# A linear attention and channel mix kernel: v cast on ScalarE, a shorter token mix, 0.5 in the relu scale, and ordered weight transfers

## The chip, the cores and the metric

The kernel runs on one core of a Trainium2 chip. The metric is the device time of one execution in microseconds (us), and what is quoted is the median of several executions. The engines are TensorE (PE in the profile, with its weight loads as PEld), VectorE (DVE), ScalarE (ACT), GpSimd (POOL) and SyncE (SP); beside them sixteen DMA engines move data.

## The reference

An efficient attention is computed for each of 8 batches and 8 heads (576 tokens, head size 64). Its output, seen as 576 x 512, goes through a channel mix that blends each token with the one before it.

```python
q_s = softmax(q, axis=-1)              # over the 64 features of a token
k_s = softmax(k, axis=2)               # over the 576 tokens
kv  = einsum('bhsd,bhse->bhde', k_s, v)
x   = einsum('bhsd,bhde->bhse', q_s, kv)          # then to (8, 576, 512)

x_prev = shift_by_one_token(x)                    # zeros in front
xk = mu_k * x + (1 - mu_k) * x_prev
xr = mu_r * x + (1 - mu_r) * x_prev
k  = relu(xk @ w_k)                               # 512 -> 1024
v  = (k * k) @ w_v                                # 1024 -> 512
r  = sigmoid(xr @ w_r)
out = r * v
```

Inputs and outputs are float32.

## The kernel before

One batch is worked in two half batches of four heads each: `attention(b, g)`. The channel mix runs in 12 units of 384 tokens: `unit(n)`. Both are generators, and the main loop interleaves them, so that TensorE works on unit n while the other engines prepare later batches. Unit 0 needs batch 0 alone; unit 1 reads tokens 384 to 767 and so needs all of batch 1 too.

Three parts matter here. First, who issues the transfers, and in which order: q, k and v from SyncE, the weights from GpSimd.

```python
def emit_load(b, g):
    t = ldpool.tile([128, 3, 2, J * D], F32, tag="raw", name="raw")
    for i, src in enumerate((q, k, v)):
        ap = ...
        nc.sync.dma_start(out=t[:, i, :, :], in_=ap)
    raw[b, g] = t

def emit_weights():
    for dst, src, n in ((wk_bf, moe_w_k, F), (wr_bf, moe_w_r, C)):
        ...                                              # four pieces each
        nc.gpsimd.dma_start(out=dst[...], in_=ap)
    for h in range(2):
        ...
        nc.gpsimd.dma_start(out=wv_h, in_=ap)
        nc.vector.tensor_scalar(out=wv_h, in0=wv_h, scalar1=0.5, scalar2=None,
                                op0=ALU.mult)
```

Second, the attention of a half batch: a cast of v on GpSimd, exps on ScalarE, the products on TensorE, and the mix on VectorE.

```python
nc.gpsimd.tensor_copy(out=vv[...], in_=t[:, 2, ...])          # v: f32 -> bf16
for i in (1, 0):                                              # k, then q
    nc.scalar.activation(out=eqk[:, i, ...], in_=t[:, i, ...], func=ACT.Exp)
# ... row sums of q, qs = q / sum; kvp = k^T v on TensorE; w = kvp / z, masked
# ... qtp = qs transposed; xp = w^T qt, one half (hf) after the other:
nc.scalar.copy(out=xb[:, hf, 64:64 + S].rearrange(...), in_=xp[:, :, 0:288])
# ... the mix, once for xk and once for xr (m):
for hf in range(2):
    c = 4 * m + 2 * g + hf
    nc.vector.tensor_scalar(out=xm[:, hf, :], in0=xb[:, hf, 64:64 + S],
                            scalar1=mu[:, c:c + 1], scalar2=None, op0=ALU.mult)
    nc.vector.tensor_scalar(out=xq[:, hf, :], in0=xb[:, hf, 0:S],
                            scalar1=om[:, c:c + 1], scalar2=None, op0=ALU.mult)
nc.vector.tensor_tensor(out=dst[...], in0=xm[:], in1=xq[:], op=ALU.add)
```

Third, a unit, and the order of the start:

```python
# in unit(n), for each of 8 column groups: four k matmuls, relu, square
nc.scalar.activation(out=rel[:], in_=kfp[:, 0:U], func=ACT.Relu)
nc.vector.tensor_tensor(out=k2[:, fc, :], in0=rel[:], in1=rel[:], op=ALU.mult)
# then three tiles of 128 tokens: rp (4 matmuls), tanh(0.5 rp), vp (8 matmuls), and
nc.vector.scalar_tensor_tensor(out=ot[:], in0=th[:], scalar=1.0, in1=vp[:],
                               op0=ALU.add, op1=ALU.mult)
# ... (sigmoid(r) = (1 + tanh(r / 2)) / 2: the halving sits in w_v)

# start (the loads of batch 0 were emitted earlier)
a0 = attention(0, 0); next(a0)
a1 = attention(0, 1); next(a1)
emit_weights()
emit_mu()
emit_load(1, 0)
emit_load(1, 1)
```

The softmax here doesn't subtract the row's maximum and nothing guards it: scores larger than these inputs give would overflow.

## Time and profile before

| | before |
|---|---|
| median of 3 executions | 246.61 us (246.5 to 248.75) |
| span of the profiled execution | 244.5 us |
| TensorE busy | 190.5 us, 78% |
| VectorE busy | 186.2 us, 76% |
| ScalarE busy | 120.0 us, 49% |
| GpSimd busy | 33.8 us, 14% |

These shares are averages over three quite different stages. The first lines are from the profile page of the kernel before: busy time per engine, and then two rows of the picture in 40 slices of about 6.1 us, in which each digit is the busy share in tenths (9 is 90% or more).

```profile
PE 190.5 (78%) x1296; PEld 103.2 (42%) x1313; DVE 186.2 (76%) x434; ACT 120.0 (49%) x197; POOL 33.8 (14%) x32
...
PE   0335200898987969797979999979999999999992
...
DVE  1489312999999999999999999999969844252521
```

TensorE is nearly idle for seven slices, to about 44 us: this is the start-up (stage 1). Then VectorE is full and TensorE has gaps (stage 2). From about 190 us TensorE alone is full (stage 3). The same in numbers, from the view that sums the engines' busy time over chosen stretches of the kernel before. A row has the stretch and its length, the busy time of each engine with its number of instructions, the granted TensorE clock as a share of full speed, the DMA share (it adds up packets that overlap, so it can pass 1) and GB/s.

```profile
core 0: us, PE busy (x) PEld busy (x) DVE busy (x) ACT busy (x) POOL busy (x), PEclk, DMA share, GB/s
24.00:44.00 20.00, 1.80 (x22) 1.38 (x23) 6.23 (x15) 5.72 (x6) 2.29 (x2) 0.57 1.11 321
...
110.00:130.00 20.00, 17.14 (x116) 9.06 (x118) 19.81 (x46) 11.83 (x19) 2.29 (x1) 1.00 0.77 249
200.00:213.00 13.00, 12.95 (x69) 6.69 (x69) 4.93 (x11) 5.72 (x11) 0.00 (x0) 1.00 0.26 61
```

In the middle (110 to 130) VectorE is 99% busy and TensorE 86%. Near the end a unit takes 13 us with TensorE at 100%. From 24 to 44 us no engine is half busy.

What the start-up waits for is read from the chain of waits of the kernel before: the work that ended last, followed back from the end, each row with its start, its length, its engine and its tile. These are its rows up to the first long run of k matmuls.

```profile
4.47 9.44 DMA raw<-in_v_dram
...
13.97 2.21 POOL vv_104 L146
16.18 0.54 POOL wk_bf L109
16.72 2.37 POOL wr_bf L109 x4
19.09 0.70 POOL wv_bf L117
19.79 21.27 DMA wv_bf<-in_moe_w_v_dram
...
41.09 0.69 DVE wv_bf L118
...
43.28 0.68 DVE xk L210
...
44.00 3.49 PE kfp L222 x11
```

The end of this chain: the second half of w_v lands, VectorE multiplies it by 0.5, and only then mixes the token rows that the first matmuls need. Its beginning: a cast of v (`vv_104`) that stood waiting for data. Rows "POOL wk_bf", "wr_bf" and "wv_bf" are GpSimd issuing transfers.

The timeline of VectorE in the kernel before shows the wait itself. A row has start, length, engine, line, operation, output and input, count, and in brackets the idle time before it and what ended that.

```profile
35.54 0.69 DVE L118 TENSOR_SCALAR wv_bf<-wv_bf 128x2048 bf16<-128x2048 bf16 x1 [8.28 <-DMA wv_bf<-in_moe_w_v_dram]
41.09 0.69 DVE L118 TENSOR_SCALAR wv_bf<-wv_bf 128x2048 bf16<-128x2048 bf16 x1 [4.85 <-DMA wv_bf<-in_moe_w_v_dram]
...
85.47 1.25 DVE L208 TENSOR_SCALAR xq<-xb_110,om 128x576 bf16<-128x576 bf16 x1
```

VectorE stood 8.28 + 4.85 = 13.1 us for 1.4 us of work. The last row is of stage 2: a scaling that takes 0.36 us elsewhere took 1.25 us, beside a cast of v on GpSimd that began at 85.28.

### The profile page before, as it was taken

The page shows a single profiled execution, that of the slowest core. Times are in us where ns is not written, and L with a number is a line of the kernel's source. Part 1 is how long each engine was busy: PE and PEld are TensorE (multiplying, and loading weights), DVE is VectorE, ACT ScalarE, POOL GpSimd, SP SyncE. Part 2 cuts the span into 40 slices and gives each one's busy share as a digit, 9 for nine tenths or more (in the row PEclk, how much of TensorE's full clock was granted, in tenths as well). Part 3 has the DMA queues.
Part 4 walks back from the last instruction along what each step waited for, and adds up shares of the span by engine and source line. Part 5 has one row for each costly group of instructions (what it writes and reads, how often), then busy time and mean ns, then how long its engine had stood idle before and what let it go on. Part 6 is the DMA issues. An engine that isn't in the chain of part 4 may idle for free.

```text
span 244.5 us, 3656 instructions
## 1 busy us (share of the span) xinstructions
PE 190.5 (78%) x1296; PEld 103.2 (42%) x1313; DVE 186.2 (76%) x434; ACT 120.0 (49%) x197; POOL 33.8 (14%) x32
## 2 busy tenths in 40 slices
PE   0335200898987969797979999979999999999992
PEld 0223200453543545453544555534655545454540
DVE  1489312999999999999999999999969844252521
ACT  4351520495292755465383774741734626162620
POOL 2375011610112010110110140100000000000000
PEclk9999655699999999999999999999999999999997
DMA  6999999921997587898881303203113031322313
GB/s 224 368 319 314 298 293 357 394 86 25 254 333 292 130 315 230 252 298 268 260 285 44 86 3 79 51 4 86 43 39 92 0 90 43 73 55 51 81 43 86
DMA packets 21065, 40.60 MB, mean 166 GB/s; under 512 B 2104, under 2 KB 3640, under 8 KB 21048
## 3 DMA queue, kind: packets, MB, share of 16 engines
q1 hardware_dynamic: 18816, 37.76, 49.4%
q0 software_dynamic: 2208, 2.62, 6.1%
q8 instruction: 10, 0.16, 0.3%
q14 instruction: 7, 0.06, 0.1%
q10 hardware_dynamic: 24, 0.00, 0.0%
HBM read 33.56 MB, written 9.44 MB: 176 GB/s over the span
## 4 chain that ended last, share of the span: by engine, by line
PE 49%; DVE 27%; DMA 14%; ACT 4%; POOL 2%; issue 1%; DVEq 0%; ACTq 0%
PE vp L239 21%; PE kfp L222 14%; PE rp L232 9%; DMA wv_bf<-in_moe_w_v_dram 9%; DVE qs L160 5%; DVE xq L208 4%; DMA raw<-in_v_dram 4%; DVE xm L206 3%; PE xp L192 2%; DVE xr L210 2%; DVE xk L210 2%; DVE rsum L156 2%; DVE ot L242 2%; ACT eqk L150 2%; PE qtp L182 2%; DMA raw<-in_q_dram 2%
## 5 line engine op out<-in xcount | busy, mean ns | idle before, releaser
L222 PE MATMUL kfp<-xk,wk_bf 128*128 128x384 bf16 x384 | 69.4, 331 | 15.9 <-DVE xk L210 15.1
L226 ACT ACTIVATE rel<-kfp 128x384 bf16<-128x384 f32 x96 | 46.1, 495 | 38.0 <-PE kfp L222 32.5
L222 PEld LDWEIGHTS <-wk_bf 128*128 128x128 bf16 x384 | 37.3, 99 | 40.0 <-issue 16.9
L150 ACT ACTIVATE eqk<-raw 128x1152 bf16<-128x1152 f32 x32 | 36.7, 1163 | 34.5 <-DMA raw<-in_q_dram 15.1
L242 DVE SCALAR_TENSOR_TENSOR ot<-th,vp 128x512 f32<-128x512 f32 x36 | 24.5, 684 | 21.7 <-PE vp L239 18.6
L235 ACT ACTIVATE th<-rp 128x512 f32<-128x512 f32 x36 | 21.6, 599 | 33.8 <-PE rp L232 33.5
L232 PE MATMUL rp<-wr_bf,xr 128*128 128x512 bf16 x130 | 36.4, 379 | 0.7
L156 DVE TENSOR_REDUCE rsum<-eqk 128x18 f32<-128x1152 bf16 x16 | 21.5, 1345 | 8.5 <-ACT eqk L150 8.5
L160 DVE TENSOR_TENSOR qs<-eqk,rrec 128x1152 bf16<-128x1152 bf16 x16 | 21.6, 1351 | 0.1
L192 PE MATMUL xp<-qt,w 128*128 128x288 bf16 x64 | 12.1, 295 | 10.2 <-DVE qt L184 6.8
L232 PEld LDWEIGHTS <-xr 128*128 128x128 bf16 x144 | 13.7, 98 | 13.3
L182 PE MATMUL qtp<-ident,qs 128*128 128x128 bf16 x144 | 11.6, 231 | 5.0 <-DVE qs L160 4.8
L146 POOL CAST vv_100<-raw 128x1152 bf16<-128x1152 f32 x6 | 8.2, 1371 | 49.3 <-PE kvp L168 42.2
L146 POOL CAST vv_108<-raw 128x1152 bf16<-128x1152 f32 x5 | 10.8, 2164 | 27.6 <-PE kvp L168 16.9
L168 PEld LDWEIGHTS <-eqk 64*128 64x128 bf16 x288 | 9.6, 102 | 11.0 <-issue 5.1
L146 POOL CAST vv_104<-raw 128x1152 bf16<-128x1152 f32 x5 | 7.7, 1547 | 44.3 <-DMA raw<-in_v_dram 22.8
L182 PEld LDWEIGHTS <-qs 128*128 128x128 bf16 x144 | 9.4, 103 | 9.5 <-DVE qs L160 7.6
L192 PEld LDWEIGHTS <-w 128*128 128x128 bf16 x64 | 6.2, 98 | 17.1 <-DVE w L175 7.4
L210 DVE TENSOR_TENSOR xr<-xm,xq 128x1152 bf16<-128x1152 bf16 x16 | 12.7, 794 | 0.0
L210 DVE TENSOR_TENSOR xk<-xm,xq 128x1152 bf16<-128x1152 bf16 x16 | 12.1, 754 | 0.0
L184 DVE COPY qt<-qtp 128x1152 bf16<-128x1152 bf16 x16 | 12.0, 747 | 0.0
L118 DVE TENSOR_SCALAR wv_bf<-wv_bf 128x2048 bf16<-128x2048 bf16 x2 | 1.4, 694 | 13.1 <-DMA wv_bf<-in_moe_w_v_dram 13.1
(78 smaller groups left out, 244.8 us busy)
## 6 DMA issues: line engine op xcount, KB each, us to landing
raw<-in_q_dram SPq DMA_DIRECT2D x16, 576.0 KB, 7.6
raw<-in_k_dram SPq DMA_DIRECT2D x16, 576.0 KB, 7.9
raw<-in_v_dram SPq DMA_DIRECT2D x16, 576.0 KB, 8.5
out_dram<-ot SPq DMA_DIRECT2D x72, 128.0 KB, 2.4
wk_bf<-in_moe_w_k_dram POOLq DMA_DIRECT2D x4, 256.0 KB, 6.8
wv_bf<-in_moe_w_v_dram POOLq DMA_DIRECT2D x2, 512.0 KB, 18.9
wr_bf<-in_moe_w_r_dram POOLq DMA_DIRECT2D x4, 128.0 KB, 8.8
mu_sb<-in_moe_mu_k_dram ACTq DMA_DIRECT2D x2, 1.0 KB
```

Of the source, the lines that this page charges most:

```text
L146: nc.gpsimd.tensor_copy(out=vv[:, :, 0:128].rearrange("p j (u d) -> p j u d", u=2), in_=t[:, 2, :, :].rearrange("p u (j d) -> p j u d", d=D))
L150: nc.scalar.activation(out=eqk[:, i, :, :, :], in_=t[:, i, :, :].rearrange("p u (j d) -> p j u d", d=D), func=ACT.Exp)
L156: nc.vector.reduce_sum(out=rsum[:], in_=eq, axis=AX.X)
L160: nc.vector.tensor_tensor(out=qs[:].rearrange("p j (u d) -> p (j u) d", u=2), in0=eq, in1=rrec[:, :, None].to_broadcast((128, 2 * J, D)), ...
L182: nc.tensor.transpose(out=qtp[:, j // 8, j % 8, :], in_=qs[:, j, :], identity=ident[:])
L192: nc.tensor.matmul(xp[:, a, 0:288], lhsT=w[:, hf, :], rhs=qt[:, hf, 288 * a:288 * a + 288], start=True, stop=True)
L210: nc.vector.tensor_tensor(out=dst[:, 2 * g:2 * g + 2, c0:c0 + S], in0=xm[:], in1=xq[:], op=ALU.add)
L222: nc.tensor.matmul(kfp[:, 0:U], lhsT=wk_bf[:, ct, fc * 128:(fc + 1) * 128], rhs=xk[:, ct, c0:c0 + U], start=(ct == 0), stop=(ct == CT - 1))
L226: nc.scalar.activation(out=rel[:], in_=kfp[:, 0:U], func=ACT.Relu)
L232: nc.tensor.matmul(rp[:], lhsT=xr[:, ct, c0 + 128 * m:c0 + 128 * m + 128], rhs=wr_bf[:, ct, :], start=(ct == 0), stop=(ct == CT - 1))
L239: nc.tensor.matmul(vp[:], lhsT=k2[:, ft, 128 * m:128 * m + 128], rhs=wv_bf[:, ft, :], start=(ft == 0), stop=(ft == FT - 1))
L242: nc.vector.scalar_tensor_tensor(out=ot[:], in0=th[:], scalar=1.0, in1=vp[:], op0=ALU.add, op1=ALU.mult)
```

## The change

Its intent: take the casts away from GpSimd, spare VectorE work, take the wait for w_v out of VectorE's order, and have the DMA engines deliver first batch 0, then the weights, then batch 1. In the kernel the mix becomes prev + mu * (cur - prev), and the 0.5 becomes a factor sqrt(0.5) in the relu, since the relu's output is squared. The core of the diff, cut:

```diff
+HALF_ROOT = 0.5 ** 0.5
+    SYNC = mybir.DependencyInfo(mybir.DependencyClass.Sync, mybir.DependencyReason.DATA)
+    def after(later, earlier):
+        if earlier is not None:
+            tc.add_manual_dep(later.ins, earlier.ins.name, SYNC)
-    def emit_load(b: int, g: int):
+    def emit_load(b: int, g: int, gate=None):
...
-            nc.sync.dma_start(out=t[:, i, :, :], in_=ap)
+            ld = nc.sync.dma_start(out=t[:, i, :, :], in_=ap)
+            after(ld, gate)
+            gate = None                      # so only q's transfer is held
...
-            nc.vector.tensor_scalar(out=wv_h, in0=wv_h, scalar1=0.5, scalar2=None,
-                                    op0=ALU.mult)
...
-        nc.gpsimd.tensor_copy(out=vv[:, :, 0:128]..., in_=t[:, 2, :, :]...)
-        for i in (1, 0):
+        for i in (0, 1):
             nc.scalar.activation(...Exp)
+        nc.scalar.copy(out=vv[:, :, 0:128]..., in_=t[:, 2, :, :]...)
...
+        nc.vector.tensor_tensor(out=xd[:], in0=xb[:, :, 64:64 + S], in1=xb[:, :, 0:S],
+                                op=ALU.subtract)
...
-                nc.vector.tensor_scalar(out=xm[:, hf, :], in0=xb[:, hf, 64:64 + S], ...mu)
-                nc.vector.tensor_scalar(out=xq[:, hf, :], in0=xb[:, hf, 0:S], ...om)
+                nc.vector.tensor_scalar(out=xm[:, hf, :], in0=xd[:, hf, :], ...mu)
-                                    in0=xm[:], in1=xq[:], op=ALU.add)
+                                    in0=xm[:], in1=xb[:, :, 0:S], op=ALU.add)
...
-            nc.scalar.activation(out=rel[:], in_=kfp[:, 0:U], func=ACT.Relu)
+            nc.scalar.activation(out=rel[:], in_=kfp[:, 0:U], func=ACT.Relu,
+                                 scale=HALF_ROOT)
...
+    wdone = emit_weights(first)              # first: v of batch 0, first half
     a0 = attention(0, 0)
...
-    emit_weights()
-    emit_load(1, 0)
-    emit_load(1, 1)
+    emit_load(1, 0, wdone[3])                # behind the last w_k transfer
+    emit_load(1, 1, wdone[7])                # behind the last w_r transfer
...
-                    emit_load(b + 1, g)
+                    emit_load(b + 1, g, wdone[-1] if b == 1 and g == 0 else None)
```

The two xp matmuls are also split at column 512 instead of 288, so that the copy from PSUM, where the products lie, reads one plain stretch, and the exp of q is written before that of k.

More of the change, by code (lines that the diff above doesn't have):

```diff
@@ L66, in emit_load @@
                          ap=[[J * D, 128], [2 * S * D, 2], [1, J * D]])
-            nc.sync.dma_start(out=t[:, i, :, :], in_=ap)
+            ld = nc.sync.dma_start(out=t[:, i, :, :], in_=ap)
+            after(ld, gate)
+            gate = None
         raw[b, g] = t
+        return ld
     mu_sb = const.tile([8, 128], F32, name="mu_sb")
@@ L76 @@
                                 .rearrange("p (u e) -> p u e", u=2), in_=ap)
-    emit_load(0, 0)
+    first = emit_load(0, 0)
     emit_load(0, 1)
@@ L100, with emit_weights @@
     wr_bf = const.tile([128, CT, C], BF16, name="wr_bf")
-    def emit_weights():
+    def emit_weights(gate):
+        done = []
         for dst, src, n in ((wk_bf, moe_w_k, F), (wr_bf, moe_w_r, C)):
@@ L108, in emit_weights @@
                                  ap=[[n, 64], [D * n, 2], [1, n]])
-                    nc.gpsimd.dma_start(out=dst[64 * u:64 * u + 64, 2 * g:2 * g + 2, :],
-                                        in_=ap)
+                    done.append(nc.gpsimd.dma_start(
+                        out=dst[64 * u:64 * u + 64, 2 * g:2 * g + 2, :], in_=ap))
+                    after(done[-1], gate)
+                    gate = None
         for h in range(2):
@@ L116, in emit_weights @@
             wv_h = wv_bf[:, h * n:(h + 1) * n, :]
-            nc.gpsimd.dma_start(out=wv_h, in_=ap)
-            nc.vector.tensor_scalar(out=wv_h, in0=wv_h, scalar1=0.5, scalar2=None,
-                                    op0=ALU.mult)
+            done.append(nc.gpsimd.dma_start(out=wv_h, in_=ap))
+        return done
     mu = const.tile([128, 8], F32, name="mu")
-    om = const.tile([128, 8], F32, name="om")
     def emit_mu():
@@ L127, in emit_mu @@
         nc.vector.tensor_copy(out=mu[:], in_=mup[:])
-        nc.vector.tensor_scalar(out=om[:], in0=mup[:], scalar1=-1.0, scalar2=1.0,
-                                op0=ALU.mult, op1=ALU.add)
     xpair = {}
@@ L144, in attention @@
         c0 = S * (b % 2)
-        nc.gpsimd.tensor_copy(out=vv[:, :, 0:128].rearrange("p j (u d) -> p j u d", u=2),
-                              in_=t[:, 2, :, :].rearrange("p u (j d) -> p j u d", d=D))
         eqk = apool.tile([128, 2, J, 2, D], BF16, tag="eqk", name="eqk")
-        for i in (1, 0):
+        for i in (0, 1):
             nc.scalar.activation(
@@ L153, in attention @@
                 func=ACT.Exp)
+        nc.scalar.copy(out=vv[:, :, 0:128].rearrange("p j (u d) -> p j u d", u=2),
+                       in_=t[:, 2, :, :].rearrange("p u (j d) -> p j u d", d=D))
         eq = eqk[:, 0, :, :, :].rearrange("p j u d -> p (j u) d")
@@ L189, in attention @@
         for hf in range(2):
-            xp = psum.tile([128, 2, 512], F32, tag="att", bufs=2, name="xp")
-            for a in range(2):
-                nc.tensor.matmul(xp[:, a, 0:288], lhsT=w[:, hf, :],
-                                 rhs=qt[:, hf, 288 * a:288 * a + 288],
+            xp = psum.tile([128, 1024], F32, tag="att", bufs=2, name="xp")
+            for c, e in ((0, 512), (512, S)):
+                nc.tensor.matmul(xp[:, c:e], lhsT=w[:, hf, :], rhs=qt[:, hf, c:e],
                                  start=True, stop=True)
-            nc.scalar.copy(out=xb[:, hf, 64:64 + S].rearrange("p (a c) -> p a c", a=2),
-                           in_=xp[:, :, 0:288])
+            nc.scalar.copy(out=xb[:, hf, 64:64 + S], in_=xp[:, 0:S])
             if hf == 0:
@@ L200, in attention @@
         yield
+        xd = apool.tile([128, 2, S], BF16, tag="xd", name="xd")
+        nc.vector.tensor_tensor(out=xd[:], in0=xb[:, :, 64:64 + S], in1=xb[:, :, 0:S],
+                                op=ALU.subtract)
         for m, dst in enumerate((xk, xr)):
             xm = apool.tile([128, 2, S], BF16, tag="xm", name="xm")
-            xq = apool.tile([128, 2, S], BF16, tag="xq", name="xq")
             for hf in range(2):
                 c = 4 * m + 2 * g + hf
-                nc.vector.tensor_scalar(out=xm[:, hf, :], in0=xb[:, hf, 64:64 + S],
+                nc.vector.tensor_scalar(out=xm[:, hf, :], in0=xd[:, hf, :],
                                         scalar1=mu[:, c:c + 1], scalar2=None, op0=ALU.mult)
-                nc.vector.tensor_scalar(out=xq[:, hf, :], in0=xb[:, hf, 0:S],
-                                        scalar1=om[:, c:c + 1], scalar2=None, op0=ALU.mult)
             nc.vector.tensor_tensor(out=dst[:, 2 * g:2 * g + 2, c0:c0 + S],
-                                    in0=xm[:], in1=xq[:], op=ALU.add)
+                                    in0=xm[:], in1=xb[:, :, 0:S], op=ALU.add)
             yield
```

## The prediction

> **What bounds the kernel now.** The profiled span, 244.5 us, has three stages (busy time by stretch).
> 1. 0 to 44 us, start-up: TensorE is busy 9 us. The DMA engines are full at about 320 GB/s: batches 0, 1 and part of 2 share them with the weights. The chain of waits runs through the second half of w_v (21.3 us, landing at 41.1), the VectorE 0.5 multiply and mix instructions to the first long k matmul run at 44.0. In-order VectorE stood 8.3 and 4.9 us before the multiplies, although its next input was done at 29.7 and w_v is not read before 53.
> 2. 44 to 190: VectorE is full until 170 (99%); TensorE idles 14 us of 146.
> 3. 190 to the end: TensorE alone, 12.97 us per 384-row unit. The change doesn't touch it.
>
> **What the change does.**
> - Removes the wv multiplies: 1.4 us of VectorE work, but 13.1 us of in-order waiting on the chain. The relu scale and the xp split should be free.
> - DMA order. The Trainium skill (DMA: Bandwidth & Descriptors, "Issuing engines are not separate DMA queues") says that queues share the 16 engines; the trace agrees: w_v took 16.5 and 21.3 us beside the batch loads. Estimated from the queue table, weights alone need 15 us, a batch 10 to 11. Then batch 0 lands by 12, wk by 18, w_v by 27, batch 1 by 36. Unit 0 can start at 24 instead of 44. But unit 1 needs all of batch 1: it starts at 46 to 48 instead of 62. Start-up: about -15 us, not -20.
> - Mix: per half batch four 128x576 scalings go (0.28 us issue to issue) and a 128x1152 subtract comes (0.67): -0.45 us, x16 = -7 us of VectorE.
> - v cast: 16 casts go from GpSimd (1.15 to 3.7 us) to ScalarE, about 1.1 us each (an exp of that size takes 1.16): ScalarE from 120 to 138 us busy. Scalings of 0.365 us median took 1.25 beside a GpSimd cast, k squares 1.2 to 1.3 instead of 0.35; I estimate 8 to 9 us in all, now gone. The Trainium skill (SBUF — State Buffer, "two separate sides") describes an exclusive lock of a shared port pair; these lengths agree.
>
> VectorE loses about 15 us in stage 2, but TensorE has only 14 us of idle there to give back, and three ScalarE passes in a row (3.3 us) can delay relu: about -7 us.
>
> Sum: 246.6 - 15 - 7 = about **224 us**, range 213 to 236. Floor: 24 us of start, 183 of remaining TensorE work, 4 of tail and launch: 211. Chances: faster by over 2% 0.93, within 2% 0.05, slower by over 2% 0.02.
>
> **What would show it right.** First long k matmul run at 22 to 28 us; no w_v wait on VectorE; weights landing before batch 1; VectorE busy 170 us, ScalarE 138, no scaling over 0.6 us; VectorE under 95% in the middle; units of 13.0 us at the end; TensorE's share of the chain well over 49%.
>
> **What would make it wrong.** Instructions may be rearranged on an engine: if ScalarE gets batch 1's exp or v cast ahead of batch 0's xb copy, or VectorE a batch 1 row sum ahead of batch 0's mix, they block until the delayed loads, and unit 0 slips to 35 or later. Weight transfers may be slower. ScalarE may become the bottleneck. Or TensorE is nearly full from 24 us on: 213.

## The result, and the profile after

The kernel after takes 229.78 us (median of 4; 229.62 to 230.54). The kernel before, run beside it on the same chip, took 247.6 us (median of 4; 246.5 to 248.75). The ratio is 0.9286, with a 95% interval of 0.9226 to 0.9346: faster by 7.1%. Ratios here are the mean time of one kernel's fast runs over that of the other's fast runs of the same rounds, so not quite the ratio of the medians quoted.

The lines of the kernel after that answer to those of before, first from its profile page.

```profile
PE 192.9 (84%) x1297; PEld 102.8 (45%) x1313; DVE 170.0 (74%) x383; ACT 135.8 (59%) x213; POOL 7.1 (3%) x16
...
PE   0245336987998899989999999999999999999991
...
DVE  0576276899999999999999999986868843333521
```

VectorE has lost 16.2 us of busy time (186.2 to 170.0), ScalarE has gained 15.8 (120.0 to 135.8). A slice is 5.7 us here. The same stretches of the kernel after:

```profile
core 0: us, PE busy (x) PEld busy (x) DVE busy (x) ACT busy (x) POOL busy (x), PEclk, DMA share, GB/s
...
24.00:44.00 20.00, 11.11 (x80) 6.21 (x79) 11.46 (x24) 11.82 (x18) 0.00 (x0) 0.66 1.06 345
...
110.00:130.00 20.00, 19.00 (x140) 10.14 (x141) 19.93 (x46) 15.03 (x26) 0.00 (x0) 1.00 0.46 137
200.00:213.00 13.00, 12.95 (x69) 6.69 (x69) 4.96 (x12) 5.74 (x12) 0.00 (x0) 1.00 0.27 62
```

In the middle TensorE went from 17.14 to 19.00 us of 20. The last stage is as it was. The start, 24 to 44 us, does more work than before (TensorE 11.11 us instead of 1.80), but is still far from full. The chain of waits of the kernel after, up to the first long run of k matmuls:

```profile
1.72 7.24 DMA raw<-in_v_dram
...
16.36 16.08 DMA wv_bf<-in_moe_w_v_dram
...
32.49 4.62 DMA raw<-in_q_dram
...
37.22 1.16 ACT eqk L157
38.38 0.39 ACT rel L233
...
38.81 2.91 PE kfp L229 x9
```

The weights land at 32.4 us instead of 41.1. The order is only partly the intended one: since only q's transfer is held, k and v of batch 1's first half were issued at 4.88 and 6.07 us, ahead of most of the weights. And now the chain goes from w_v to a *load of q that was told to wait for w_v* (at 32.49), through the exp of that q, to the relu.

To place the gain I use one measure throughout: the end of unit n is the start of the third output tile (`ot`) of that unit on VectorE, in the profiled execution.

| | end of unit 0 | end of unit 8 | units 0 to 8 | end of unit 11 |
|---|---|---|---|---|
| before | 62.8 | 200.8 | 138.0 | 239.8 |
| after | 54.8 | 185.1 | 130.3 | 224.0 |
| difference | -8.0 | | -7.7 | -15.8 |

The last three units take 38.9 us in both (before rounding). So about half of the gain comes from the start and half from the middle. (The spans differ by 15.7 us, the medians by 17.8; the profiled execution of before was near the fast end of its range, that of after the slowest of its four.) The prediction had -15 for the start and -7 for the middle.

### The profile page after: what moved, and what is told of

It is laid out like the page before. It is cut to its first block, busy times and chain, and to the rows that moved or that the text cites. A ratio compares the mean times of both kernels' runs of the same rounds, so it can differ in the third digit from the quotient of the medians.

```text
span 228.8 us, 3599 instructions
## 1 busy us (share of the span) xinstructions
PE 192.9 (84%) x1297; PEld 102.8 (45%) x1313; DVE 170.0 (74%) x383; ACT 135.8 (59%) x213; POOL 7.1 (3%) x16
## 4 chain that ended last, share of the span: by engine, by line
PE 52%; DMA 17%; DVE 16%; ACT 5%; issue 3%; POOL 2%; SPq 1%; DVEq 0%; ACTq 0%; POOLq 0%
PE vp L247 20%; PE kfp L229 16%; PE rp L240 10%; DMA wv_bf<-in_moe_w_v_dram 7%; DMA raw<-in_v_dram 6%; DVE ot L250 3%; PE xp L201 2%; DVE rsum L165 2%; ACT eqk L157 2%; DMA raw<-in_q_dram 2%; DVE xm L215 2%; DVE qt L193 2%; DMA raw<-in_k_dram 2%; PE qtp L191 2%; PE kvp L177 2%
## 5 line engine op out<-in xcount | busy, mean ns | idle before, releaser
L229 PE MATMUL kfp<-xk,wk_bf 128*128 128x384 bf16 x384 | 72.0, 338 | 4.1 <-DVE xk L217 3.6
L229 PEld LDWEIGHTS <-wk_bf 128*128 128x128 bf16 x384 | 37.3, 101 | 31.5 <-issue 8.7
L215 DVE TENSOR_SCALAR xm<-xd,mu 128x576 bf16<-128x576 bf16 x64 | 20.7, 366 | 0.1
L177 PEld LDWEIGHTS <-eqk 64*128 64x128 bf16 x288 | 9.8, 102 | 24.0 <-issue 16.3
L201 PE MATMUL xp<-qt,w 128*128 128x512 bf16 x64 | 12.0, 295 | 6.1 <-DVE qt L193 6.1
L177 PE MATMUL kvp<-vv_100,eqk 64*128 64x129 bf16 x108 | 4.9, 233 | 10.2 <-ACT vv_100 L161 10.2
L191 PE MATMUL qtp<-ident,qs 128*128 128x128 bf16 x144 | 12.1, 236 | 1.2 <-DVE qs L169 1.2
L191 PEld LDWEIGHTS <-qs 128*128 128x128 bf16 x144 | 10.0, 106 | 5.1 <-DVE qs L169 2.4
L203 ACT CAST xb_110<-xp 128x576 bf16<-128x576 f32 x10 | 6.3, 638 | 7.6 <-PE xp L201 7.6
L184 DVE SCALAR_TENSOR_TENSOR w<-kvp,rz,mask 128x128 bf16<-128x128 f32 x32 | 9.8, 342 | 0.2
L177 PE MATMUL kvp<-vv_108,eqk 64*128 64x129 bf16 x90 | 4.0, 236 | 6.9 <-ACT xb_106 L203 6.9
L161 ACT CAST vv_100<-raw 128x1152 bf16<-128x1152 f32 x6 | 7.0, 1163 | 1.9 <-DMA raw<-in_v_dram 1.8
## 6 DMA issues: line engine op xcount, KB each, us to landing
wv_bf<-in_moe_w_v_dram POOLq DMA_DIRECT2D x2, 512.0 KB, 14.7
```

The lines of the kernel that those rows point to most:

```text
L177: nc.tensor.matmul(kvp[:, hf, 0:129], lhsT=eqk[r, 1, j, :, :].rearrange("p u d -> p (u d)"), rhs=vv[r, j, 0:129], start=(j == 0), stop=(j ...
L191: nc.tensor.transpose(out=qtp[:, j // 8, j % 8, :], in_=qs[:, j, :], identity=ident[:])
L201: nc.tensor.matmul(xp[:, c:e], lhsT=w[:, hf, :], rhs=qt[:, hf, c:e], start=True, stop=True)
L215: nc.vector.tensor_scalar(out=xm[:, hf, :], in0=xd[:, hf, :], scalar1=mu[:, c:c + 1], scalar2=None, op0=ALU.mult)
L229: nc.tensor.matmul(kfp[:, 0:U], lhsT=wk_bf[:, ct, fc * 128:(fc + 1) * 128], rhs=xk[:, ct, c0:c0 + U], start=(ct == 0), stop=(ct == CT - 1))
```

## The experiments

The theory, called A in the texts: in-order engines decide the start. What the start gained, it gained by taking a wait out of VectorE's order (the w_v multiplies). What it didn't gain, it lost in ScalarE's order: exps of batch 1, whose loads are now held back by the dependencies, stand ahead of copies and relus that unit 0 needs. So the dependencies gain nothing as they are, and would gain something with another order on ScalarE (this last part is called D). The main rival: the transfers alone decide the start, since batch 1 and the weights arrive too late whatever the order. For the middle, the theory called M is that the casts on GpSimd cost it time by slowing VectorE; its rival is that the mix brings what the middle gains. Where a text uses another letter, it means one of these rivals.

The timeline of ScalarE, and two rows of TensorE, in the kernel after are what A rests on.

```profile
24.24 0.73 PE L201 MATMUL xp<-qt,w 128*128 128x512 bf16 x4
...
35.73 2.72 PE L229 MATMUL kfp<-xk,wk_bf 128*128 128x384 bf16 x8 [1.61 <-DVE xk L217]
...
27.14 1.16 ACT L157 ACTIVATE eqk<-raw 128x1152 bf16<-128x1152 f32 x1 [5.47 <-DMA raw<-in_q_dram]
30.15 1.16 ACT L157 ACTIVATE eqk<-raw 128x1152 bf16<-128x1152 f32 x1 [1.85 <-DMA raw<-in_k_dram]
31.22 1.16 ACT L203 CAST xb_106<-xp 128x576 bf16<-128x576 f32 x2
...
37.22 1.16 ACT L157 ACTIVATE eqk<-raw 128x1152 bf16<-128x1152 f32 x1 [1.80 <-DMA raw<-in_q_dram]
38.29 1.61 ACT L233 ACTIVATE rel<-kfp 128x384 bf16<-128x384 f32 x4
```

The matmuls of batch 0's second half were done at 24.97, and their copy out of PSUM ran at 31.22, behind two exps of batch 1 for which ScalarE waited 5.47 and 1.85 us. The first relus ran at 38.29, behind an exp of batch 2. The Trainium skill, in "TensorE: Matmul & The Clock Gate", section "Architectural detail: the array is 16× 32×32, not 1× 128×128", says that ScalarE and VectorE work their queues strictly first in, first out; these rows agree.

### Only the 0.5 folded into the relu, on the kernel before

```diff
-            nc.vector.tensor_scalar(out=wv_h, in0=wv_h, scalar1=0.5, scalar2=None,
-                                    op0=ALU.mult)
...
-            nc.scalar.activation(out=rel[:], in_=kfp[:, 0:U], func=ACT.Relu)
+            nc.scalar.activation(out=rel[:], in_=kfp[:, 0:U], func=ACT.Relu,
+                                 scale=HALF_ROOT)
```

> The kernel before, with only the 0.5 moved from the two w_v multiplies into the relu scale. Theory A (most of the start-up gain is the in-order wait of VectorE for w_v, 13.1 us in the kernel before): no VectorE wait for w_v, the first long k matmul run at 31 to 34 us instead of 44.0, time 236 to 242, ratio to before 0.955 to 0.98. Rival B (the start-up gain comes from the order of the transfers): the run starts after 40 and the ratio is above 0.985.

Measured: 238.85 us (238.39 to 239.74) beside 248.12 of before, ratio 0.9639 (0.956 to 0.9718). The before runs include one of 427.7 us, which counts as a slow one and is left out of the ratios. The long k run began at 32.71 us. Unit 0 ended at 56.4, and units 0 to 8 took 136.2. So on the kernel before, the fold alone takes 6.4 us from the start, as A has it.

### The kernel after without its dependencies

```diff
-        if earlier is not None:
+        if False:
             tc.add_manual_dep(later.ins, earlier.ins.name, SYNC)
```

> The changed kernel without its manual dependencies (weights and loads issued as the program order gives them). Theory A: the dependencies are worth little, because they also delay q of batch 1, behind which ScalarE holds batch 0's second copy (it had its input at 24.97 and ran at 31.22): within 3 us of the changed kernel, ratio to before 0.915 to 0.945. Rival B: at least 5 us slower than the changed kernel, ratio above 0.95, with the first long k matmul run later than 40.

Measured: 230.03 us, ratio 0.9279 (0.9206 to 0.9352), against 0.9286 for the kernel after. Unit 0 ended at 55.1 (54.8 with them). The dependencies do change the order: with them batch 0's first half reached xb at 17.87 instead of 24.16. And they give it all back: the long k run began at 38.81 with them and 38.06 without. In the kernel after they are worth nothing that these runs can tell (the intervals are 1.8 us either way).

### The kernel after with the casts back on GpSimd

```diff
-        nc.scalar.copy(out=vv[:, :, 0:128]..., in_=t[:, 2, :, :]...)
+        nc.gpsimd.tensor_copy(out=vv[:, :, 0:128]..., in_=t[:, 2, :, :]...)
```

> The changed kernel with the v cast back on GpSimd. Theory (GpSimd casts stretch VectorE instructions that meet them, and that stretch was on the critical path of the middle stage): VectorE instructions of over 1.1 us that should take 0.37 come back, VectorE busy 175 to 180 us instead of 170.0, time 234 to 239, ratio 0.945 to 0.965. Rival (what VectorE gains, ScalarE's extra 18 us take back): within 2 us of the changed kernel, ratio 0.92 to 0.937.

Measured: 246.79 us, ratio 0.994 (0.9862 to 1.0018). The expectation was missed by some 8 us: undoing this one part loses the whole gain. The busy time of VectorE, 180.0 us, was as expected; the start was not: unit 0 ended at 69.5, 14.7 us later than in the kernel after. Rows of its GpSimd, TensorE and VectorE timelines show two waits.

```profile
16.50 0.75 POOL L130 DMA_DIRECT2D wv_bf<-in_moe_w_v_dram  x1 [2.17 <-DMA wk_bf<-in_moe_w_k_dram]
17.24 2.25 POOL L161 CAST vv<-raw 128x1152 bf16<-128x1152 f32 x2
...
18.45 1.16 PE L177 MATMUL kvp<-vv,eqk 64*128 64x129 bf16 x18 [9.25 <-POOL vv L161]
...
33.14 1.12 PE L201 MATMUL xp<-qt,w 128*128 128x512 bf16 x4 [12.45 <-DVE qt L193]
...
28.65 1.35 DVE L165 TENSOR_REDUCE rsum<-eqk 128x18 f32<-128x1152 bf16 x1 [13.77 <-ACT eqk L157]
```

GpSimd works in order too (the same page of the Trainium skill has it so for each of GpSimd's cores), and in the changed kernel the weight transfers are issued ahead of the casts. The first cast had to wait until the last weight transfer was issued, at 17.24 us, and the first kvp matmuls came at 18.45 instead of 10.19: 8.3 us. The second wait is a held load again. TensorE then stood 12.45 us for VectorE's copy qt of batch 0, and that copy stood behind a row sum of batch 1, for which VectorE waited 13.77 us: its exp needed the q that is held behind w_k. The parts of the change are therefore not independent; what each of the two waits costs alone was not tried. This run says nothing clean about what the casts cost in the middle (units 0 to 8 took 131.6 us, but with a start so late more attention was done before unit 0 ended), so that was tried apart, below.

### ScalarE's order changed: batch 1 behind batch 0's copies

An ordering without a semaphore is added on ScalarE: the exps and the cast of half batch n stand behind the copies to xb of half batch n - 2, and those of batch 1 behind the last copy of batch 0.

```diff
+        me = box[0]                        # number of this half batch
...
+            behind(ex, copies.get(me - (1 if me == 2 else 2)))
...
+        behind(ca, copies.get(me - (1 if me == 2 else 2)))
...
+            copies[me] = nc.scalar.copy(out=xb[:, hf, 64:64 + S], in_=xp[:, 0:S])
```

> The changed kernel, with ScalarE's order of instructions alone changed: exps and cast of half batch n only behind the copies to xb of half batch n-2 (for the first half of batch 1: n-1). Theory A (in the changed kernel ScalarE stands before an exp whose load is held back, and the copy of batch 0 and the first relu wait behind it): copy of batch 0's second half at about 25 instead of 31.2, first long k matmul run at 27 to 30 instead of 38.8, unit 1 at 48 to 53 instead of 57, time 221 to 226, ratio 0.89 to 0.915. Rival C (the start-up is bound by the transfers, since unit 1 needs all of batch 1): unit 0 starts sooner but unit 1 still at 56 to 58, time within 2 us of 229.8.

Measured: 228.94 us, ratio 0.9234 (0.9158 to 0.9311). The expectation missed. The k matmuls that need batch 0's second half began at 27.22 (35.73 in the kernel after), but unit 0 still ended only at 53.3: ScalarE now stood 2.24 us for the held load of batch 1's *second* half, until 32.58, and only then came to the first relus, at 33.65. The wait had moved by one step.

### The casts on GpSimd from batch 2 on only

This leaves the start of the kernel after alone and puts the casts of the middle back.

```diff
+        cast = nc.scalar.copy if b < 2 else nc.gpsimd.tensor_copy
+        cast(out=vv[:, :, 0:128]..., in_=t[:, 2, :, :]...)
```

> The changed kernel with the v cast on GpSimd from batch 2 on only; the start-up keeps ScalarE's cast, so that no cast stands behind the weight transfers on GpSimd's queue (as the first casts did in the kernel with all casts on GpSimd, where the first one ran at 17.2 us). Stage 2 is the time from the end of unit 0 (its third output tile) to the end of unit 8: 138.0 us before, 130.3 in the changed kernel, 131.6 with all casts on GpSimd. Theory M (the stretched VectorE instructions were most of the 7.7 us of stage 2): stage 2 at 134 to 137, time 233.5 to 237. Rival N (VectorE has enough slack after the mix is shortened; the loss of the all-GpSimd kernel was the start-up queue): stage 2 at 130 to 132, time within 2 us of 229.8.

Measured: 237.85 us, ratio 0.9599 (0.9556 to 0.9643); the time is a little over the range. Unit 0 ended at 55.4 and units 0 to 8 took 136.9 us, 6.6 more than after. VectorE was busy 177.6 us instead of 170.0. So the casts in the middle cost about 8 us of time. They cost it through VectorE: in units 0 to 8 the profile lists 10.5 us in which TensorE waited, all of it for VectorE and none for a cast; in the kernel after it lists 5.0. Two rows of this run's timelines of GpSimd and VectorE show how:

```profile
67.11 1.95 POOL L162 CAST vv<-raw 128x1152 bf16<-128x1152 f32 x1 [3.08 <-PE vp L248]
...
67.97 1.25 DVE L216 TENSOR_SCALAR xm<-xd,mu 128x576 bf16<-128x576 bf16 x1
```

Both are stretched where they overlap: casts on GpSimd took 1.14 to 3.74 us in the kernel before, a scaling takes 0.37 us alone. Here the scaling ended at 69.22, just after the cast (69.06); in the pair shown of the kernel before the ends are 86.72 and 86.57. The Trainium skill, "SBUF — State Buffer", section "🔬 SBUF: two separate sides", describes an exclusive lock on a port pair that VectorE and GpSimd share, and says that ScalarE's port waits for nobody; the runs agree: in both pairs the scaling ended 0.15 to 0.16 us after the cast, as if it had waited for it, and on ScalarE the casts took 1.13 to 1.25 us.

### The kernel after with the old mix

```diff
-                nc.vector.tensor_scalar(out=xm[:, hf, :], in0=xd[:, hf, :], ...mu)
+                nc.vector.tensor_scalar(out=xm[:, hf, :], in0=xb[:, hf, 64:64 + S], ...mu)
+                nc.vector.tensor_scalar(out=xq[:, hf, :], in0=xb[:, hf, 0:S], ...om)
...
-                                    in0=xm[:], in1=xb[:, :, 0:S], op=ALU.add)
+                                    in0=xm[:], in1=xq[:], op=ALU.add)
```

> The changed kernel with the mix as it was (mu*cur + (1-mu)*prev, two scalings and an add per half). VectorE gets back 0.45 us per half batch, about 6 us in stage 2. If VectorE still bounds stage 2: stage 2 at 133.5 to 136, time 233 to 236. If TensorE already bounds it: stage 2 at 130 to 132, time within 2 us of 229.8, VectorE busy about 177 us.

Measured: 233.65 us, ratio 0.9427 (0.9384 to 0.947). The total is as expected, 3.9 us over the kernel after, with VectorE at 175.4 us (5.4 more). Where it lies was missed: 2.6 us at the start and only 0.6 in units 0 to 8. Against the rival of M: the mix is the smaller part, and hardly in the middle.

### ScalarE's order changed for both halves of batch 1

```diff
-            behind(ex, copies.get(me - (1 if me == 2 else 2)))
+            behind(ex, copies.get(me - (1 if me in (2, 3) else 2)))
```

(The same for the cast.)

> As the run with ScalarE reordered, but both half batches of batch 1 are held behind the copies to xb of the half batch before, so that no relu of unit 0 stands behind an exp of the second half of batch 1 (there the second pair of relus waited until 33.6). Theory A (start-up is bound by what ScalarE waits for in order): the first relus at about 30.4, six of them before 36, unit 0 ends at 48 to 51 instead of 53.3, time 224 to 227. Rival C (start-up bound by the transfers of batch 1 and the weights): unit 0 ends no earlier than 52.5, or unit 1 waits for batch 1 and its end (70.8) does not move; time within 1.5 us of 228.9.

Measured: 226.36 us (226.09 to 226.6), ratio 0.9134 (0.9084 to 0.9184). Unit 0 ended at 49.2, 5.6 us earlier than in the kernel after, by ordering alone, with the same dependencies. In its ScalarE timeline the copies run at 23.77 and the relus at 30.47 (31.22 and 38.29 in the kernel after):

```profile
23.77 1.18 ACT L213 CAST xb<-xp 128x576 bf16<-128x576 f32 x2 [5.94 <-PE xp L211]
...
30.47 0.86 ACT L243 ACTIVATE rel<-kfp 128x384 bf16<-128x384 f32 x2
```

The middle takes 1.4 us longer (131.7); why was not tried. The total, 229.78 against 226.36 us, is 3.4 better, as A expected.

### Batch 1 computed from batch 0's tiles

This kernel is wrong (relative error 0.465): batch 1 isn't loaded at all, which takes 3.5 MB from the start and frees ScalarE of the waits for batch 1. One transfer of batch 2 still waits for w_v.

```diff
-        t = raw.pop((b, g))
+        t = raw[(max(b, 1) - 1 if b < 2 else b, g)]
...
-    emit_load(1, 0, wdone[3])
-    emit_load(1, 1, wdone[7])
```

> The changed kernel with batch 1 computed from batch 0's tiles, so that its 3.5 MB are not transferred (the output of batch 1 is wrong on purpose). The order of instructions is nearly kept. If the transfers bound the start-up (C): the copy of batch 0's second half at about 20 to 24 instead of 31.2, unit 0 ends at 43 to 48 instead of 54.8, time 216 to 223. If something else does (the slow TensorE clock after idling, the chain of half batches on VectorE and ScalarE): unit 0 ends at 50 or later, time above 225.

Measured: 225.03 us, ratio 0.9076 (0.9027 to 0.9124). Unit 0 ended at 50.2, between what the theories expected. If the transfers of batch 1 were what held the start (the rival), taking them away should have done more than reordering ScalarE (49.2) did. Rows of its ScalarE and TensorE timelines show what was left:

```profile
31.61 1.16 ACT L157 ACTIVATE eqk<-raw 128x1152 bf16<-128x1152 f32 x1 [5.88 <-DMA raw<-in_q_dram]
...
34.26 1.61 ACT L233 ACTIVATE rel<-kfp 128x384 bf16<-128x384 f32 x4
...
34.78 1.76 PE L229 MATMUL kfp<-xk,wk_bf 128*128 128x384 bf16 x5 [4.24 <-ACT rel L233]
```

ScalarE stood 5.88 us for the q of batch 2, whose load waits for w_v; the relus came behind it, and TensorE, with all its inputs there, stood 4.24 us for a relu. So even without batch 1's transfers it was ScalarE's order. The transfers still count through the held load: w_v landed at 27.8 us here and at 32.4 in the kernel after, 4.6 us earlier, and unit 0 ended 4.6 us earlier too. The slow TensorE clock that the expectation also names is small beside this: the five matmuls after the wait took 0.35 us each, the next eleven 0.20.

### The kernel after, again

The same kernel, to have it on the chip of the next two.

> The changed kernel once more, unaltered, so that the two next runs can be compared with it on one chip: ratio to before 0.923 to 0.934.

Measured: 230.05 us beside 247.25 of before, ratio 0.9318 (0.9279 to 0.9358); unit 0 ended at 54.1, units 0 to 8 took 130.3.

### ScalarE's order changed, and no dependencies

The ordering of both halves of batch 1, with `if False:` in the dependencies as in the second experiment.

> The faster reordered kernel (both half batches of batch 1 held on ScalarE behind the copies before them), with all manual dependencies of the change taken away. Theory D (the dependencies bring batch 0 in about 6 us sooner, copies to xb at 17.9 against 24.2 us, and the changed kernel loses that again because ScalarE stands before the held-back loads; with ScalarE reordered their gain shows): slower than the reordered kernel with the dependencies by 2.5 to 5 us, time 229 to 231.5, unit 0 ends at 52 to 55 instead of 49.2. Rival E (the dependencies are worth nothing whatever the order, since all bytes must arrive anyway): within 1 us of 226.4.

Measured: 228.76 us, ratio 0.9255 (0.9224 to 0.9286); unit 0 ended at 51.7, just short of the expected range. With ScalarE's order mended, the dependencies are worth 228.76 - 226.36 = 2.4 us by medians (on two chips; the ratios, 0.9255 and 0.9134, make it 3.0 of 247.4). In the kernel after they were worth nothing: the two parts need each other.

### ScalarE's order changed, one dependency less

In the ordered kernel, the first half of batch 1 isn't held behind w_k any more.

```diff
-    emit_load(1, 0, wdone[3])
+    emit_load(1, 0)
```

> The faster reordered kernel with one dependency fewer: q of the first half of batch 1 no longer waits for w_k (its k and v did not wait in the changed kernel either). ScalarE stood 2.4 us before this load in the reordered kernel; so if that wait was still on the path: unit 0 ends at 45 to 48, time 223.5 to 225.5. If the bytes only change places (w_k and w_v come that much later): within 1 us of 226.4.

Measured: 223.74 us (223.61 to 224.8), ratio 0.9057 (0.9027 to 0.9087): 6.3 us faster than the kernel after on the same chip, 5.0 faster than the ordered kernel without any dependency there, correct, and the fastest of all. Unit 0 ended at 46.5, units 0 to 8 took 131.7. Its ScalarE timeline has relus at 27.66, waiting for matmuls and no longer for loads:

```profile
27.66 1.13 ACT L243 ACTIVATE rel<-kfp 128x384 bf16<-128x384 f32 x2 [0.39 <-PE kfp L239]
```

### Only the cast moved, on the kernel before

The last run asks what the casts alone are worth.

```diff
-        nc.gpsimd.tensor_copy(out=vv[:, :, 0:128]..., in_=t[:, 2, :, :]...)
...
+        nc.scalar.copy(out=vv[:, :, 0:128]..., in_=t[:, 2, :, :]...)
```

> The kernel before with the v cast moved to ScalarE and nothing else (w_v multiplies, old mix and no dependencies stay). Theory: the cast is worth 6 to 7 us of stage 2 (end of unit 0 to end of unit 8: 138.0 us before) also by itself, and nothing at the start, where VectorE still stands before w_v: no VectorE instruction that should take 0.37 us takes over 1.1, first long k matmul run still at 42 to 45, stage 2 at 131 to 133, time 239.5 to 242. Rival (the gain of the cast needs the shorter mix, else VectorE bounds stage 2 as before): stage 2 at 135 or more, time above 243.

Measured: 233.94 us (232.75 to 234.49) beside 248.41, ratio 0.9426 (0.9397 to 0.9456): 14.5 us, far more than expected. Units 0 to 8 took 130.2 us, a little under the expected range (7.8 less than before), and no scaling took over 0.37 us. The surprise is the start: the long k run began at 37.73 instead of 44.0, and unit 0 ended at 56.8, 6.0 us earlier, though the w_v multiplies are still there. Its timelines of GpSimd and VectorE:

```profile
8.00 0.77 POOL L117 DMA_DIRECT2D wv_bf<-in_moe_w_v_dram  x1 [1.53 <-DMA wk_bf<-in_moe_w_k_dram]
10.06 0.74 POOL L117 DMA_DIRECT2D wv_bf<-in_moe_w_v_dram  x1 [1.29 <-DMA wk_bf<-in_moe_w_k_dram]
...
31.53 0.69 DVE L118 TENSOR_SCALAR wv_bf<-wv_bf 128x2048 bf16<-128x2048 bf16 x1 [0.30 <-DMA wv_bf<-in_moe_w_v_dram]
```

In the kernel before, GpSimd issued w_v at 19.0 us, behind two casts that waited for v (9.45 and 13.97). Without casts in its queue it issues w_v at 8.00 and 10.06; w_v lands at 31.5 instead of 41.1, and VectorE waits 0.3 us for it instead of 13.1. This is the beginning of the chain shown for the kernel before.

## Why the prediction was right or wrong

The time, 229.78 us, lies in the range of 213 to 236, and "faster" came true. The sum behind it was half right; that the total still fell within the range owes something to the range's width, 23 us.

**The failed step is the start-up term of the sum: "Start-up: about -15 us", with unit 0 starting at 24 and unit 1 at 46 to 48.** It measured -8.0. The first eight k matmuls (half of the sums of four column groups, all that batch 0's first half allows) did run at 21.73, but the next eight came at 35.73, the long run at 38.81 and the end of unit 0 at 54.8. The estimate reckoned when the data would land and took the engines to be ready for it. (The landing was off too: w_v at 32.4, not 27.) In its place the runs showed that ScalarE, in order, stood before exps whose loads the new dependencies hold back. Ordering alone brought 5.6 us back at the start (49.2); ordering with one dependency less brought 8.3 (46.5). That is 16.3 us under the kernel before: the -15 was there to be had, but not in this instruction order. The prediction named this among what would make it wrong ("unit 0 slips to 35 or later"), and gave it no share of the number. What bounds the start of the fastest kernel was not tried.

**The middle, -7 us: measured -7.7.** The size was right, in part by luck. The mix was counted with the casts, and the runs part them: the casts of the middle are worth about 8 us in total, the mix 3.9 us, of which 2.6 lie at the start and 0.6 in units 0 to 8. VectorE time saved by the mix is thus mostly not time saved in the middle. A full VectorE was not by itself the limit there: from 110 to 130 us it was 100% busy with the old mix and with only the cast moved, and yet TensorE's listed waits in units 0 to 8 were 4.8 and 5.1 us in these two, as in the kernel after (5.0). With casts on GpSimd they were 10.5, and 11.8 in the kernel before. How exactly a saving divides between start and middle stays rough, because how much attention is done when unit 0 ends differs from run to run.

**The end, 0: measured 0** (38.9 us for three units in both).

**The w_v wait.** The prediction saw VectorE's wait and put its cause to the full DMA engines. The runs show two ways to remove it, each worth about 6 us at the start: don't touch w_v on VectorE (-6.4), or issue it earlier by taking the casts out of GpSimd's queue (-6.0, although batch 0 then lands later: its last v at 20.15 us instead of 13.91). Done together they can't both count. A sum worked out from the runs: 6 for this wait, 8 for the casts of the middle and 3.9 for the mix is 17.9, against 17.8 measured; so close a fit is partly chance, since the end of unit 0 alone differed by 0.7 us between two profiles of the kernel after. The fold on top of the moved cast was not run alone, so that it adds nearly nothing there is an inference from the 0.3 us of wait that was left.

**The order of the transfers.** The prediction counted on the dependencies for its start-up. They were worth 0 in the kernel after and 2 to 3 us once ScalarE's order was mended. The one on batch 1's first half cost about 2 us (ratios 0.9134 with it and 0.9057 without, on two chips); without that one, the rest were worth 5.0 us on one chip (228.76 against 223.74).

**The signs.** Right: VectorE 170.0 us (170 said), ScalarE 135.8 (138), no wait for w_v on VectorE, no scaling over 0.6 us (0.37 at most), units of 13.0 us. The relu with a scale takes 495 ns, as without. Wrong: the first long k run at 38.81 (22 to 28 said); VectorE in the middle stayed at 99% (under 95% said), and TensorE's share of the chain of waits rose from 49 to 52%, hardly "well over".

## What to carry to other kernels

An instruction queue is a resource like any other: before holding back a transfer, look at which engine's next instruction will wait for it, and at what stands behind that instruction. The same goes for transfers issued from an engine that also computes: they leave only when the work ahead of them is done. And follow a chain of waits to its beginning; a late landing may be a late issue.

## What the Trainium skill lacked or had wrong

- "DMA: Bandwidth & Descriptors", section "Issuing engines are not separate DMA queues", says that issuing from several engines saves only sequencer time, "which is usually small relative to the DMA itself". It lacks that an issue also waits for the compute work ahead of it in the issuing engine's queue. Here that was large: w_v was issued at 19.0 us behind casts on GpSimd and at 8.00 without them, landed at 41.1 and 31.5, and the start was 6.0 us shorter. The reverse holds too: casts behind weight issues began at 17.24 us, and the first products that need them came 8.3 us later (18.45 instead of 10.19).
- "TensorE: Matmul & The Clock Gate", section "Architectural detail: the array is 16× 32×32, not 1× 128×128", states the strict order of ScalarE and VectorE; no page draws the conclusion that delaying a load can cost more than it frees. Here one such dependency cost about 2 us in the reordered kernel, and in the kernel after a copy ready at 24.97 us ran at 31.22 behind an exp that waited for a delayed load.
- "SBUF — State Buffer", section "🔬 SBUF: two separate sides", has the lock, but no figure for what it costs a kernel with interleaved work. Here 12 casts of 128x1152 moved to ScalarE were worth about 8 us of 238, against 1.13 to 1.25 us of ScalarE each.
- The same TensorE page warns in "Seeing it yourself" that recorded clock events can be unreliable, without such a case as this: in the kernel without dependencies the granted clock is recorded as 1.00 from 24 to 44 us, while 13 matmuls of 128x384 from 38.06 on took 4.32 us (0.33 each) and 11 from 43.07 on took 1.95 (0.18 each). That the first ran at a slower clock is inferred from these lengths.
